# A fused attention and two-layer MLP kernel: wider conversion of second-layer weights, float32 scores of two heads, one mask on VectorE

## The chip, the core and the metric

The kernel runs on one core of a Trainium2 chip. The metric is the device time of one execution in microseconds (us), as the median of several runs. One profiled execution gives the trace. TensorE is PE in the profile (PEld its weight loads), VectorE is DVE, ScalarE ACT, GpSimd POOL, and SyncE, which issues the transfers, SP. Each engine works through its instructions in the order in which the program emits them.

## The reference

Three stages follow one another on 4 x 576 = 2304 tokens of width 512:

```python
scores = q @ k.T / 8                          # 4 batches, 8 heads, 576 x 576, head_dim 64
scores = where(0 <= i - j < 128, scores - slope[h] * |i - j|, -1e9)
x = softmax(scores) @ v                       # heads side by side: 2304 x 512
h = x @ w_in;  x = (h * clip(h + 3, 0, 6) / 6) @ w_out          # d_ff 2048
h = x @ w_in2; out = (s * max(h, 0)**2 + b) @ w_out2            # d_ff 2048
```

All inputs are float32. The weights arrive as 64-bit values (two 32-bit words each), and the kernel turns them into float32 itself.

## The kernel before

**Order of the work.** Everything is entered into a table `plan` by `at(slot, rank, fn)`. At the end the functions are called by slot, and within a slot by rank. This order is the order on every engine; nothing moves an instruction later. Two slots belong to one step `(t, f)` of the first layer: token group `t` (0 to 7; groups 0 to 3 have 256 tokens, the first two query blocks of a batch; groups 4 to 7 have 320, the other three blocks) and 128 columns `f` of d_ff (0 to 15). `hslot` and `oslot` (L80 to L83) give the slots of a step's two products. Groups 0 and 1 are interleaved; group 2 begins at slot 77, group 3 at 109, group 4 at 141, 5 at 173, 6 at 205, 7 at 237 (`last`), and the second layer at 271 (`base`).

**First layer.** A product in near-float32 precision is made of three products of float32r parts: each operand is a rounded part and a remainder. `Step.h` (L597) makes 12 instructions into the single PSUM bank `h`; `relu` on ACT (L608), `product` on DVE (L611), `hi` on ACT (L618) and `lo` on DVE (L622) make the operand of `Step.o` (L635), again 12 instructions, one step later. The next step's `h` needs the bank, which is free once `product` has read it. `Step.end` sends a group's result to DRAM (`x2d`). First-layer weights are converted by `Half` in slots up to about 70.

**Attention.** It runs ahead of the first layer: the eight heads of group g are spread over the 32 slots that end some four slots before group g begins, four slots to a head. For groups 0 and 1 (`StartUnit`) a float32 product on 64 partitions for each of two heads makes the scores (L501). For the others (`Unit`) ACT rounds scaled queries and keys (`casts`, L306 and L307), DVE and POOL make the remainders (`rests`, L311, L316), and two float32r products on 128 partitions make each square of scores (L335). Then: minimum on DVE (L351, L352), exponential on ACT (L362), normalization on POOL (L378), transposition on PE (L387), copy on ACT (`fold`, L391), and the two triangles of each 128 x 128 block by selects on POOL (`masks`, L403). The product with the values (L418) and its rounding (L429, L433) come once for two heads. Score, transpose and value tiles take turns in PSUM banks by `bank` (L131): three of them from slot 23 on.

**Second-layer weights.** The second layer multiplies by a scheme of seven block products, so the weights are not only converted but also combined. One `Pair` (L682) handles 2 x 128 rows of `w_in2` or `w_out2`; there are 16. ACT extracts two parts (L720, L721), DVE shifts and merges the sign (L725, L728), POOL adds (L734), DVE makes four sums (L759), then four times ACT rounds (L770), DVE or POOL makes the remainder (L774), and a store sends both to DRAM (`wh`, `wo`, L784). All use two input buffers in turn and a single `work` tile. The rounded parts are written back into the input buffer, two halves in turn, so the third rounding overwrites what the first store sends. Starts are 7 slots apart, four in each of the groups 3 to 6 (L1100).

**Second layer.** `Tokens` loads `x2d` (L841), forms differences on POOL (L861) and splits them on ACT and DVE (L870, L871). `Inner` and `Tokens.outer` stream the stored weights through a ring of five tiles (`Chunk`) and make the products (L1034, L955). For its first 768 tokens load and splits are planned during group 7.

Of the kernel before, what the change touches and what calls it, by code (L numbers as in the profile page):

```python
# [17 lines left out]
P = 128  # L18
# [5 lines left out]
def tile_alibi_window_attention_moe_moe2(  # L24
# [34 lines left out]
    wpool = layer1.enter_context(tc.tile_pool(name="wpool", bufs=1, side="right"))  # L59
# [27 lines left out]
    warm = wpool.tile([P, 512], BF16, tag="w7", name="warm")  # L87
# [13 lines left out]
    rel0 = rel2[:, P:]  # L101
    s_sb = const.tile([P, 1], F32, name="s_sb")
    b_sb = const.tile([P, 1], F32, name="b_sb")

    def constants():
# [16 lines left out]
        make_identity(nc, ident)  # L122

# [34 lines left out]
    class Half:  # L158
# [18 lines left out]
        def load(self):  # L177
            if self.stage is None:
                raw = raw_half()
            else:  # L180
                raw = wpool.tile(
                    [P, 4 * DM], I32, tag=f"w{self.stage}", name=f"stage{self.id}"
                )[:, : 2 * DM]
# [24 lines left out]
        def hi(self):  # L208
            if self.f not in wt:
                wt[self.f] = wpool.tile(  # L210
                    [P, 2, 2 * DM], F32R, tag=f"w{self.f}", name=f"w1_{self.f}"
                )
# [31 lines left out]
    queries = {}  # L244
    for x in "XY":
        queries[x] = [ap.tile([P, 3 * P], F32R, tag=f"q{x}{i}", bufs=1, name=f"q{x}{i}") for i in (0, 1)]
        for t in queries[x]:
            nc.gpsimd.memset(t[:, S - 2 * P :].bitcast(F32), 0.0)

    def query_tile(x):  # L250
        queries[x].reverse()
        return queries[x][0]

    class Unit:
# [10 lines left out]
        def plan(self, s):  # L265
            two = min(self.qa + 2, self.qb)
            at(s - 7, 1, self.load)
            at(s - 1, 34, self.casts)
            at(s + 1, 33, self.rests)
            at(s + 3, 20, lambda: self.products(self.qa, two))  # L270
            at(s + 4, 20, lambda: self.products(two, self.qb))
            at(s + 3, 32, lambda: self.minima(self.qa, two))
            at(s + 4, 32.7, lambda: self.minima(two, self.qb))
            at(s + 5, 33, lambda: self.exps(self.qa, two))
            at(s + 5, 33, lambda: self.exps(two, self.qb))
            at(s + 6, 32.2, self.sums)
            at(s + 7, 33, self.weights)
            at(s + 9, 20, self.transposes)
            at(s + 9, 35, self.fold)
            at(s + 10, 30.02, self.masks)  # L280
            if self.h % 2:
                at(s + 13, 20, self.values)
                at(s + 14, 39, self.to_hi)
                at(s + 15, 39, self.to_lo)
# [4 lines left out]
        def load(self):  # L289
            i, b = (1, self.b) if self.qa else (0, self.b - NATIVE)  # L290
            raw = ap.tile([P, 768], F32, tag="raw", name=f"raw{self.id}")[:, : self.nq + self.nk]
            nc.sync.dma_start(out=raw, in_=qk[i][b, self.h])
            self.rq = raw[:, : self.nq]
            self.rk = raw[:, self.nq :]
            if self.h % 2 == 0:
                rv = ap.tile([P, 2, 4 * D], F32, tag="v", bufs=3, name=f"rv{self.id}")
                rv = rv[:, :, : self.nkb * D]
                nc.sync.dma_start(out=rv, in_=vv[i][b, self.h // 2])
                for u in self.pair():
                    u.rv = rv[:, u.h % 2].rearrange("p (n d) -> p n d", d=D)  # L300

        def casts(self):
            self.c = -(D ** -0.5) / slopes[self.h]
            self.X = query_tile("X")
            self.C = ap.tile([P, 448], F32R, tag="C", name=f"C{self.id}")[:, : self.nk]
            nc.scalar.activation(self.X[:, : self.nq], self.rq, AF.Copy, scale=self.c)  # L306
            nc.scalar.activation(self.C, self.rk, AF.Copy)  # L307

        def rests(self):
            self.Y = query_tile("Y")  # L310
            nc.vector.scalar_tensor_tensor(  # L311
                out=self.Y[:, : self.nq], in0=self.rq, scalar=self.c,
                in1=self.X[:, : self.nq].bitcast(F32),
                op0=ALU.mult, op1=ALU.subtract,
            )
            nc.gpsimd.tensor_tensor(  # L316
                out=self.C[D:], in0=self.rk[D:], in1=self.C[D:].bitcast(F32), op=ALU.subtract
            )
# [7 lines left out]
        def products(self, a, b):  # L326
            if a == self.qa:
                self.ps = []
            if a < b:
                self.ps.append(bank(f"s{self.id}_{a}"))  # L330
            for i in range(a, b):
                sl, k0, k1 = self.square(i)
                q = (i - self.qa) * P
                for x in (self.X, self.Y):
                    nc.tensor.matmul(  # L335
                        sl,
                        lhsT=x[:, q : q + P],
                        rhs=self.C[:, k0 - self.ka * P : k1 - self.ka * P],
                        start=x is self.X,
                        stop=x is self.Y,  # L340
# [51 lines left out]

# [832 lines left out]
```

## Time and profile before

| | |
|---|---|
| median of 3 runs | 1001.66 us (995.66 to 1003.28) |
| profiled execution | 998.22 us, its span in the trace 996.5 us |
| mean granted TensorE clock | 0.976 of full speed |
| busy: PE, DVE, ACT, POOL | 914.9, 705.5, 529.0, 528.9 us |

The busy time of an engine is summed over the whole span. Matmuls are pipelined, so that a product which waits in the pipe counts as busy. "Idle before, releaser" in a row is the time for which the engine stood still before the instruction, with the instruction that ended it. The granted clock is the share of full speed (2.4 GHz) at which the chip let TensorE run in a stretch.

Where rows are cut by time, the columns are: stretch in us, its length, busy us of PE, PEld, DVE, ACT and POOL (each with its instructions), granted clock, share of the DMA engines, GB/s. The stretches of rows 1 begin with the first `h` product of a token group.

### The profile page before, as it was taken

The numbers are of one execution on the slowest core, as the hardware profiler recorded it, in microseconds if no ns is written. First come the engines' busy times: TensorE is split into PE (matmuls) and PEld (weight loads), VectorE is DVE, ScalarE is ACT, GpSimd is POOL, SyncE is SP. The second block draws the span as 40 slices with busy tenths as digits, with TensorE's granted clock in tenths as the row PEclk, the third lists the DMA queues.
The fourth block names the chain that finished last, engine by engine and source line by source line (L and its number), as shares of the span: only waits on it lengthen the run. The fifth ranks groups of instructions, "written<-read, shape, count | busy, mean of one in ns | idle before, by whom it ended". The sixth has DMA issues, their size and how long they took to land.

```text
span 996.5 us, 18129 instructions
## 1 busy us (share of the span) xinstructions
PE 914.9 (92%) x6517; PEld 868.1 (87%) x6517; DVE 705.5 (71%) x1489; ACT 529.0 (53%) x1283; POOL 528.9 (53%) x685
## 2 busy tenths in 40 slices
PE   9898999997788889878899989999799997999998
PEld 4697899996778878768788989999699997999998
DVE  7999975566766667577675462778956789667693
ACT  7977864455555555546555332555324554336541
POOL 6646753445775576477554130338922479223772
PEclk9999999999989999899999999999999999999999
DMA  9425532244655555454734610987379873797863
GB/s 332 138 77 189 170 96 66 79 136 156 217 176 185 206 176 200 159 178 141 243 135 172 252 59 1 341 282 256 125 266 342 280 276 108 269 326 243 275 227 133
DMA packets 61130, 191.50 MB, mean 192 GB/s; under 512 B 6384, under 2 KB 17776, under 8 KB 52592
## 3 DMA queue, kind: packets, MB, share of 16 engines
q1 hardware_dynamic: 61040, 190.34, 55.6%
q8 instruction: 51, 0.84, 0.3%
q14 instruction: 39, 0.32, 0.1%
HBM read 151.52 MB, written 38.80 MB: 191 GB/s over the span
## 4 chain that ended last, share of the span: by engine, by line
PE 56%; DVE 16%; DMA 10%; ACT 7%; POOL 6%; issue 4%; SPq 1%; ACTq 0%; POOLq 0%; DVEq 0%
PE h L1034 17%; PE o L955 14%; PE h L597 12%; PE o L635 9%; DMA wh<-raw 3%; DVE i L938 3%; DVE work L759 2%; DMA raw<-w 2%; POOL P L378 2%; DMA wo<-raw 2%; PE v L418 2%; POOL work L734 2%; ACT P L362 1%; POOL W L403 1%; DVE g L622 1%
## 5 line engine op out<-in xcount | busy, mean ns | idle before, releaser
L597 PE MATMUL h<-x,w 128*128 128x256 f32 (+1 forms) x1536 | 239.8, 307 | 37.0 <-DVE t L611 36.4
L597 PEld LDWEIGHTS h<-x,w 128*128 128x128 f32 x1536 | 220.7, 197 | 44.6 <-DVE t L611 43.4
L635 PE MATMUL o<-g,w 128*128 128x256 f32 (+1 forms) x1536 | 235.2, 302 | 10.1 <-ACT g L618 5.8
L635 PEld LDWEIGHTS o<-g,w 128*128 128x128 f32 x1536 | 213.3, 192 | 14.6 <-ACT g L618 7.9
L955 PE MATMUL o<-wstream,i 128*128 128x256 f32 x1512 | 184.8, 284 | 13.8 <-DVE i L938 13.5
L955 PEld LDWEIGHTS o<-wstream,i 128*128 128x128 f32 x1512 | 183.0, 192 | 15.4 <-DVE i L938 15.4
L1034 PE MATMUL h<-x,wstream 128*128 128x384 f32 x864 | 154.2, 335 | 0.0
L1034 PEld LDWEIGHTS h<-x,wstream 128*128 128x128 f32 x864 | 150.4, 188 | 0.0
L403 POOL TENSOR_SCALAR_AFFINE_SELECT W<-F 128x128 f32<-128x128 f32 (+1 forms) x240 | 78.3, 364 | 116.1 <-ACT F L391 114.5
L622 DVE TENSOR_TENSOR g<-t,g 128x256 fp32r<-128x256 f32 (+1 forms) x128 | 74.1, 579 | 59.8 <-ACT g L618 59.6
L608 ACT ACTIVATE t<-h 128x256 f32<-128x256 f32 (+1 forms) x128 | 52.1, 407 | 115.1 <-PE h L597 115.0
L611 DVE SCALAR_TENSOR_TENSOR t<-t,h 128x256 f32<-128x256 f32 (+1 forms) x128 | 57.4, 449 | 69.0 <-ACT t L608 68.4
L938 DVE TENSOR_TENSOR i<-g,i 128x768 fp32r<-128x768 f32 x60 | 95.7, 1650 | 6.0 <-issue 4.9
L770 ACT ACTIVATE raw<-work 128x512 fp32r<-128x512 f32 x64 | 36.6, 573 | 97.1 <-DVE work L759 55.6
L949 POOL TENSOR_TENSOR g<-g 128x768 f32<-128x768 f32 x36 | 86.5, 2428 | 0.0
L378 POOL TENSOR_SCALAR P<-P,st 128x128 f32<-128x128 f32 x128 | 67.5, 542 | 3.7 <-DVE st L372 1.9
L1067 POOL TENSOR_TENSOR g<-g 128x384 f32<-128x384 f32 x24 | 22.6, 940 | 82.8 <-ACT g L1063 82.8
L618 ACT ACTIVATE g<-t 128x256 fp32r<-128x256 f32 (+1 forms) x128 | 56.1, 438 | 19.5 <-DVE t L611 19.4
L1071 ACT ACTIVATE g<-g,b_sb,s_sb 128x384 f32<-128x384 f32 x96 | 62.7, 698 | 3.8 <-DVE g L1058 3.8
L316 POOL TENSOR_TENSOR C<-raw,C 64x448 fp32r<-64x448 f32 (+1 forms) x48 | 53.0, 1103 | 15.1 <-issue 6.3
L1079 POOL TENSOR_TENSOR i<-g,i 128x384 fp32r<-128x384 f32 x24 | 24.8, 1034 | 67.2 <-ACT i L1075 67.2
L1058 DVE SCALAR_TENSOR_TENSOR g<-g 128x384 f32<-128x384 f32 x72 | 55.6, 772 | 2.5
(115 smaller groups left out, 1413.6 us busy)
## 6 DMA issues: line engine op xcount, KB each, us to landing
wstream<-wo SPq DMA_DIRECT2D x42, 1024.0 KB, 4.9
raw<-w SPq DMA_DIRECT2D x53, 512.0 KB, 5.6
wstream<-wh SPq DMA_DIRECT2D x24, 1024.0 KB, 5.5
wstream<-wh SPq DMA_DIRECT2D x24, 768.0 KB, 5.6
raw<-qk SPq DMA_DIRECT2D x32, 384.0 KB, 3.1
wh<-raw SPq DMA_DIRECT2D x24, 512.0 KB, 4.6
wo<-raw SPq DMA_DIRECT2D x24, 512.0 KB, 3.3
stage<-w SPq DMA_DIRECT2D x11, 512.0 KB, 5.7
```

The costliest lines, as they stand in the source:

```text
L378: nc.gpsimd.tensor_scalar(out=pt, in0=pt, scalar1=self.st[:, 2, li : li + 1], scalar2=1.0, op0=ALU.mult, op1=ALU.mult,)
L403: nc.gpsimd.affine_select(out=self.W[:, o : o + r], in_=self.F[:, q : q + r], fill=0.0, base=k - 1, compare_op=ALU.is_ge, pattern=[[s, r]] ...
L597: nc.tensor.matmul(self.ps, lhsT=w[:, wp, cc * P : (cc + 1) * P], rhs=x[:, cc, xp], start=m == 0, stop=m == 3 * CC - 1,)
L611: nc.vector.scalar_tensor_tensor(out=self.a, in0=self.a, scalar=6.0, in1=self.ps, op0=ALU.min, op1=ALU.mult)
L618: nc.scalar.activation(self.g[:, 0], self.a, AF.Copy)
L622: nc.vector.tensor_tensor(out=self.g[:, 1], in0=self.a, in1=hi, op=ALU.subtract)
L635: nc.tensor.matmul(acc[t][d], lhsT=w[:, wp, DM + d * P : DM + (d + 1) * P], rhs=self.g[:, gp], start=f == 0 and i == 0 and (t > 1 or d % 2 ...
L938: nc.vector.tensor_tensor(out=out[:, :, 1], in0=src, in1=out[:, :, 0].bitcast(F32), op=ALU.subtract)
L949: nc.gpsimd.tensor_tensor(out=out, in0=a, in1=b, op=op)
L955: nc.tensor.matmul(self.acc[k][c], lhsT=g[:, gp, c * P : (c + 1) * P], rhs=w[:, wp * HB : (wp + 1) * HB], start=p == 0 and i == 0, stop=p ...
L1034: nc.tensor.matmul(ps, lhsT=w[:, wp, cc], rhs=x[:, cc, xp], start=start and m == 0, stop=m == 5, skip_group_check=True,)
L1071: nc.scalar.activation(g, g, AF.Identity, scale=s_sb, bias=b_sb)
```

## The change

- **Conversion (`Pair`).** Its steps are spread over nine slots after its start instead of seven, each in a slot of its own, with ranks of 37 and above for the late ones (behind the step's own instructions at 30 to 32). Starts are 10 slots apart; the first two are at slots 76 and 96, the other 14 from slot 113 to 243. The first two stores leave from a staging buffer of their own (in the attention's pool, at the end in `x1`); only the third and fourth write into the input buffer. DVE makes the first and third remainder, POOL the second and fourth (the other way round before), and the order of the four parts changes.
- **Scores of groups 2 to 7.** Queries and keys of two heads lie on the two halves of the partitions. ACT scales both heads' queries in one instruction, and float32 products on 64 partitions make the scores. The casts and remainders are gone. A pair of heads is planned together, with the odd head's later steps one or two slots after the even head's. Values are loaded on their own, later.
- **Masks.** The lower triangle of the first two blocks of a unit is made by one DVE product of the transposed weights in PSUM with a constant triangle of ones. The other selects stay on POOL.
- **Pools.** First-layer weights 0 to 7 lie in a pool that closes after step (7, 7); tokens, their splits and the fifth ring tile are placed accordingly. `Step.end` writes from tiles `y` of its own, not from conversion buffers. `W` has 3 buffers (4 before), `v` 2 (3 before). The first four weight chunks are loaded from slot 253 on (240 before), the load of the second layer's first tokens is planned at slot 238 (245 before) and their splits are spread out.

```diff
         def plan(self, s):
             two = min(self.qa + 2, self.qb)
...
+            odd = self.h % 2
+            s -= 4 * odd
+            if not odd:
+                at(s - 7, 1, self.load)
+                at(s + 1, 1, self.load_values)
+                at(s - 1, 34, self.scale)
+                at(s + 3, 20, lambda: self.scores(self.qa, two))
+                at(s + 7, 20, lambda: self.scores(two, self.qb))
+            at(s + 3 + 2 * odd, 32, lambda: self.minima(self.qa, two))
+            at(s + 7 + odd, 32.7, lambda: self.minima(two, self.qb))
+            at(s + 5 + odd, 33, lambda: self.exps(self.qa, two))
+            at(s + 8 + odd, 33, lambda: self.exps(two, self.qb))
+            at(s + 9 + odd, 32.2, self.sums)
+            at(s + 10 + odd, 33, self.weights)
+            at(s + 12 + 2 * odd, 20, self.transposes)
+            at(s + 12 + 2 * odd, 35, self.fold)
+            at(s + 12 + 2 * odd, 35, self.lower)
+            at(s + 13 + 2 * odd, 30.02, self.masks)
+            if odd:
+                at(s + 17, 20, self.values)
...
         def load(self):
...
+            n = (self.qb - self.qa) * P
+            raw = ap.tile([P, 832], F32, tag="raw", name=f"raw{self.id}")[:, : n + self.nk]
+            if self.nq < n:
+                nc.gpsimd.memset(raw[:, self.nq : n], 0.0)
+            for u in self.pair():
+                u.p = slice((u.h % 2) * D, (u.h % 2 + 1) * D)
+                src = qk[i][b, u.h, u.p]
+                nc.sync.dma_start(out=raw[u.p, n:], in_=src[:, self.nq :])
+                nc.sync.dma_start(out=raw[u.p, : self.nq], in_=src[:, : self.nq])
...
+        def scale(self):
+            j = self.h // 2
+            nc.scalar.activation(self.q, self.q, AF.Copy, scale=qscale[:, j : j + 1])
...
-                for x in (self.X, self.Y):
+                for u in self.pair():
+                    sl, k0, k1 = u.square(i)
+                    q = (i - self.qa) * P
                     nc.tensor.matmul(
...
+                        sl, lhsT=u.X[:, q : q + P], rhs=u.rk[:, k0 - self.ka * P : k1 - self.ka * P],
+                        start=True, stop=True,
                     )
...
+        def lower(self):
+            self.W = ap.tile([P, 640], F32, tag="W", bufs=3, name=f"W{self.id}")
+            w = self.W[:, : 4 * P].rearrange("p (i k n) -> p i k n", i=2, k=2)
+            ps = self.pt[:, : 2 * P].rearrange("p (i n) -> p i n", i=2)
+            nc.vector.tensor_tensor(
+                out=w[:, :, 1], in0=ps, in1=tri[:, None, :].to_broadcast([P, 2, P]), op=ALU.mult
+            )
...
 class Pair:
...
         def plan(self, s, load):
+            self.s = s
             at(load, 1, self.load)
             at(s, 30.1, self.high)
-            at(s, 38, self.sign)
-            at(s + 1, 31, self.add)
-            at(s + 2, 31.2, self.sums)
+            at(s + 1, 30.1, self.rest)
+            at(s + 1, 38, self.shift)
+            at(s + 2, 38, self.sign)
+            at(s + 3, 31, self.add)
+            at(s + 4, 37, lambda: self.sums(0))
+            at(s + 5, 37, lambda: self.sums(2))
...
-                k = s + (2, 3, 5, 6)[j]
+                k = s + (4, 5, 7, 8)[j]
                 idx = [order.index(x) for x in products]
-                at(k, 31.3, lambda a=(j, src): self.hi(*a))
-                at(k + 1, 31.4, lambda a=(j, src): self.lo(*a))
-                at(k + 1, 31.5, lambda a=(j, idx): self.store(*a))
+                at(k, 37.3, lambda a=(j, src): self.hi(*a))
+                at(k + 1, 37.4, lambda a=(j, src): self.lo(*a))
+                at(k + 1, 37.5, lambda a=(j, idx): self.store(*a))
...
+        def target(self, j, n):
+
+            whole = staging(self.s) if j < 2 else self.raw.bitcast(F32)
+            return whole[:, j % 2 * 2 * DM : j % 2 * 2 * DM + n * DM]
...
-            (nc.gpsimd, nc.vector)[j % 2].tensor_tensor(
+            (nc.vector, nc.gpsimd)[j % 2].tensor_tensor(
                 out=lo.bitcast(F32R), in0=src, in1=hi, op=ALU.subtract
             )
...
-    starts = [hslot[t, 0] + 5 + 7 * i for t in range(3, 7) for i in range(4)]
+    first = hslot[3, 0] + 4
+    starts = [76, 96] + [first + 10 * i for i in range(2 * NP - EARLY)]
     for i, s in enumerate(starts):
-        Pair(i, i % NP, i // NP).plan(s, max(s - 5, starts[i - 2] + 8 if i > 1 else 0))
+        Pair(i, i % NP, i // NP).plan(s, s - 5)
...
         if t == 0:
-            p = last + 10
-            u.plan_input(last + 8, [p, p + 1, p + 2, p + 4, p + 6, p + 8, base + 1], [p + 2, p + 3, p + 5, p + 7])
+            load, p = last + 1, last
+            splits = {1: 5, 5: 9, 7: 13, 3: 20, 6: 24, 2: 25, 4: 29}
+            sums = {5: 7, 7: 10, 6: 21, 4: 26}
...
-    ready = (last + 3, last + 3, last + 4, last + 5, base + 1)
+    done = starts[-1] + 10
+    half = oslot[nt1 - 1, NF // 2 - 1] + 2
+    ready = (done, done, done, done, max(done, half))
```

## Rows read from the trace of the kernel before

**Rows 1.** Busy time (instructions) by engine, PEclk granted clock; cut at token groups 2 to 7

```profile
155.95:211.58 55.63, 55.63 (x474) 53.88 (x473) 30.22 (x115) 28.54 (x100) 23.34 (x58) 1.00 0.27 85
211.58:296.34 84.76, 69.00 (x523) 63.72 (x522) 59.77 (x166) 45.55 (x129) 53.39 (x91) 0.92 0.52 174
296.34:384.71 88.37, 75.98 (x523) 71.52 (x521) 61.46 (x168) 49.05 (x134) 55.93 (x92) 0.96 0.53 182
384.71:475.44 90.73, 77.37 (x522) 72.35 (x521) 61.94 (x167) 49.20 (x134) 56.80 (x92) 0.94 0.53 181
475.44:556.58 81.14, 72.60 (x494) 68.41 (x493) 51.77 (x125) 43.69 (x108) 41.92 (x68) 0.96 0.50 175
556.58:626.15 69.57, 66.44 (x434) 65.63 (x433) 32.28 (x49) 22.35 (x47) 9.92 (x5) 0.98 0.32 114
```

**Rows 2.** The same view, two stretches of groups 0 and 1

```profile
31.42:77.00 45.58, 41.29 (x323) 36.64 (x322) 43.92 (x98) 38.44 (x92) 20.85 (x25) 1.00 0.37 116
77.00:155.95 78.95, 74.21 (x598) 69.18 (x596) 65.30 (x179) 60.03 (x169) 50.26 (x78) 1.00 0.45 139
```

**Rows 3.** Waits, 211.58 to 618 us: engine and line, releaser, total us, times, longest

```profile
ACT raw L770 <- DVE work L759: 55.6, 16, 4.9
...
PE h L597 <- DVE t L611: 32.4, 18, 3.9
ACT raw L770 <- DMA wh<-raw: 25.1, 10, 3.8
...
ACT raw L770 <- DMA wo<-raw: 16.4, 10, 4.0
```

**Rows 4.** The chain that ended last, 296.3 to 330 us: start us, us, what

```profile
305.71 1.77 PE h L597 x12
...
313.34 1.86 POOL work L734
...
315.85 1.24 DVE work L759 x3
...
317.54 3.53 PE h L597 x12
...
324.23 4.60 DMA wh<-raw
```

**Rows 5.** Groups of instructions, whole span: count, busy us, mean ns, idle before

```profile
L403 POOL TENSOR_SCALAR_AFFINE_SELECT W<-F 128x128 f32<-128x128 f32 (+1 forms) x240 | 78.3, 364 | 116.1 <-ACT F L391 114.5 <-ACT g L618 1.1
...
L316 POOL TENSOR_TENSOR C<-raw,C 64x448 fp32r<-64x448 f32 (+1 forms) x48 | 53.0, 1103 | 15.1 <-issue 6.3 <-POOL P L378 6.0
...
L311 DVE SCALAR_TENSOR_TENSOR qY<-raw,qX 128x320 fp32r<-128x320 f32 (+1 forms) x48 | 34.6, 720 | 0.0
...
L759 DVE TENSOR_TENSOR work<-work 128x256 f32<-128x256 f32 x64 | 33.1, 546 | 14.8 <-POOL work L734 13.7
...
L774 DVE TENSOR_TENSOR raw<-work,raw 128x512 fp32r<-128x512 f32 (+1 forms) x32 | 24.1, 753 | 1.6 <-ACT raw L770 1.5
...
L728 DVE SCALAR_TENSOR_TENSOR raw<-raw,work 128x1024 int32<-128x1024 int32 x16 | 19.7, 1232 | 0.5
...
L433 DVE TENSOR_TENSOR x<-v,x 128x256 fp32r<-128x256 f32 (+1 forms) x32 | 14.4, 449 | 0.0
...
L725 DVE TENSOR_SCALAR work<-work 128x1024 int32<-128x1024 int32 x16 | 11.5, 718 | 3.8 <-ACT work L720 3.6
```

**Rows 6.** Instructions in order of time at the two kinds of score products

```profile
8.64 0.93 PE L501 MATMUL s<-raw 64*128 64x128 f32 x8
9.50 1.90 PE L93 MATMUL warm_ps<-warm 128*128 128x512 bf16 x8
...
249.51 0.33 SPq L292 DMA_DIRECT2D raw<-qk  x1
249.54 0.39 PE L335 MATMUL s<-C,qX 128*128 128x256 f32 x1 [1.42 <-POOL C L316]
...
250.12 1.10 PE L635 MATMUL o<-g,w 128*128 128x256 f32 x8
```

More of the change, by code (lines that the diff above doesn't have):

```diff
@@ L122, in constants @@
         make_identity(nc, ident)
+        nc.gpsimd.memset(tri, 1.0)
+        nc.gpsimd.affine_select(
+            out=tri, in_=tri, fill=0.0, compare_op=ALU.is_ge, base=0,
+            pattern=[[1, P]], channel_multiplier=-1,
+        )
+        for h in range(H):
+            c = -(D ** -0.5) / slopes[h]
+            nc.gpsimd.memset(qscale[h % 2 * D : (h % 2 + 1) * D, h // 2 : h // 2 + 1], c)
     def scalars():
@@ L266, in plan @@
             two = min(self.qa + 2, self.qb)
[L267 to L284, printed above, removed]
+            odd = self.h % 2
[18 more added lines that the diff above has]
+                at(s + 17, 20, self.values)
+                at(s + 18, 39, self.to_hi)
+                at(s + 19, 39, self.to_lo)
         def pair(self):
@@ L324, in square, with scores @@
             return self.ps[(i - self.qa) // 2][:, o : o + k1 - k0], k0, k1
[L326 to L330, printed above, removed]
+        def scores(self, a, b):
+            for u in self.pair():
+                if a == self.qa:
+                    u.ps = []
+                if a < b:
+                    u.ps.append(bank(f"s{u.id}_{a}"))
             for i in range(a, b):
-                sl, k0, k1 = self.square(i)
-                q = (i - self.qa) * P
-                for x in (self.X, self.Y):
+                for u in self.pair():
+                    sl, k0, k1 = u.square(i)
+                    q = (i - self.qa) * P
                     nc.tensor.matmul(
[L336 to L340, printed above, removed]
+                        sl, lhsT=u.X[:, q : q + P], rhs=u.rk[:, k0 - self.ka * P : k1 - self.ka * P],
+                        start=True, stop=True,
                     )
@@ L669, in work, with staging @@
         return late["work"]
+    def staging(s):
+        k = "early" if s + 6 < last else "late"
+        assert k == "early" or s + 4 >= last
+        if k not in late:
+            pool, tag = (ap, "stage") if k == "early" else (xpool, "x1")
+            late[k] = pool.tile([P, 4 * DM], F32, tag=tag, bufs=1, name=f"staging_{k}")
+        return late[k]
     HORDER = (1, 5, 6, 7, 3, 2, 4)
@@ L740, in block, with sums @@
             return t[:, i * DM + j * HB : i * DM + (j + 1) * HB]
[L742 removed]
+        def sums(self, first):
             L, S = ({(i, j): self.block(x, i, j) for i in (0, 1) for j in (0, 1)} for x in "LS")
@@ L829, in load @@
         def load(self):
-            if self.t == 0:
-                self.raw = [
-                    wpool.tile([P, 2, TT], F32, tag=f"w{i}", name=f"xr0_{i}") for i in (0, 1)
-                ]
-            else:
-                self.raw = late["xr"]
+            self.raw = late["xr"]
             a = self.t * TT
@@ L876, in plan_input @@
             at(load, 1, self.load)
-            for s, product in zip(splits, FORMS):
+            for product, s in splits.items():
                 at(s, 72.2, lambda n=product: self.split(n))
-            for s, product in zip(sums, (5, 7, 6, 4)):
+            for product, s in sums.items():
                 at(s, 72.5, lambda n=product: self.sum(n))
@@ L1133, in tile_alibi_window_attention_moe_moe2, with tiles, blocks, tokens_pool @@
         at(chunks[before].last + 1 if before >= 0 else ready[c.i], 0.5, c.load)
-    def late_pool():
-        attn_ctx.close()
-        pool = ctx.enter_context(tc.tile_pool(name="late", bufs=1, reuse_waits="tile"))
-        late["xb"] = {k: pool.tile([P, 2, 2, N2], F32R, name=f"x{k}", tag=f"x{k}") for k in FORMS[:-1]}
-        late["t4"] = pool.tile([P, 2, N2], F32, name="t4")
+    def tiles(pool, n, name, shape, dtype=F32):
+        return [pool.tile([P, *shape], dtype, name=f"{name}{i}", tag=f"{name}{i}") for i in range(n)]
+    def blocks(pool, products):
+        for k in products:
+            late["xb"][k], = tiles(pool, 1, f"x{k}_", (2, 2, N2), F32R)
+    def tokens_pool():
+        attn_ctx.close()
+        pool = ctx.enter_context(tc.tile_pool(name="tokens", bufs=1, reuse_waits="tile"))
+        late["xr"] = tiles(pool, 2, "xr", (2, TT))
+        late["xb"] = {}
+        blocks(pool, (1, 5, 7, 6))
+    def more_pool():
+        first_weights.close()
+        late["p"] = ctx.enter_context(tc.tile_pool(name="more", bufs=1, reuse_waits="tile"))
+        blocks(late["p"], (3, 2, 4))
     def second_pool():
```

141 lines of the change are left out of this document (51 added, 90 removed).

## The prediction

> **What bounds the kernel now.** I began with the busy times of all engines in stretches cut at the first `h` product of each token group. PE is the engine that has to be kept busy, but what it loses differs by stretch [rows 1]. Group t=2 takes 55.63 us with PE busy in all of it, at a granted clock of 1.00. Group t=3 runs the same 16 steps on as many tokens and takes 84.76 us, of which PE is busy in 69.00, at 0.92. The difference is that the conversion of second-layer weights (`Pair`) begins there. No other engine is full in t=3 to t=6: DVE is busy for 59.77 of 84.76 us and 61.46 of 88.37, ACT and POOL for less. So the loss is an order of waits, not a lack of engine time.
>
> The loss is idle time of PE plus (1 - granted clock) x stretch, since after idling PE is granted less clock and the next 12 products take 3.53 us where 12 of the same kind took 1.77 shortly before [rows 4]. From rows 1: t=3 15.8 + 6.8 = 22.5 us; t=4 12.4 + 3.5 = 15.9; t=5 13.4 + 5.4 = 18.8; t=6 8.5 + 3.2 = 11.8; t=7 3.1 + 1.4 = 4.5. **Together 73.5 us.** It is a low figure, because a product that waits counts as busy: t=3 lies 29.1 us above t=2, of which its wider scoring explains some 4 by estimate (a third tile for each of 8 heads, at 0.29 us for its two score instructions [rows 6] and as much again for its transpose and values), so 25 against the 22.5. I take 76, and 83 as the upper end (2.5 more in each of four groups).
>
> The waits say why [rows 3]. PE waits 32.4 us for `t` at L611, the DVE product that frees the single bank `h`. Behind that stands ACT, in order: it waits 55.6 us at L770 for the sums of L759, and 25.1 + 16.4 us at the same line until a store of the half it is about to overwrite has landed. The chain shows it [rows 4]: ACT does L720 and L721 back to back, POOL adds at L734, DVE sums, and only then comes the DVE product that PE stands for; a little later a store of 4.60 us holds L770, and everything queued behind it on ACT.
>
> **The change, part by part.**
>
> *Conversion.* The chain of one `Pair` is spread from 7 slots to 9, a step per slot, with 10 slots between starts instead of 7, and its late steps get ranks behind the step's own relu, product and rounding. The first two stores leave from a separate staging buffer, so no write waits for a store of its own conversion: the 41.5 us of DMA waits at L770 go. The 55.6 us go if the sums, a slot ahead now, are done when ACT comes to L770; what is late next is then POOL's add, which waits for the sign step at the end of the slot before. Two conversions move to t=2 and two into t=7. The count of instructions is the same; DVE gets the first and third rounding remainder, POOL the second and fourth. DVE spends (33.1 + 19.7 + 11.5 + 24.1)/16 = 5.5 us on a conversion [rows 5], and a remainder of 512 columns in place of one of 256 adds about 0.5.
>
> *Scores.* Per head the casts and remainders go: DVE 34.6 us, POOL 53.0 us over 48 heads [rows 5], and two ACT copies for each head, of which one scale per pair comes back; ACT is nowhere the fullest engine in rows 1, so I price it at nothing. On PE four instructions that make two squares of one head take 0.58 us from their first start to the start of what follows, so 1.16 for two heads. The start-up units already do float32 products of two heads: 8 instructions for 768 columns take 0.86 us [rows 6], so 1024 columns about 1.15. Nothing is gained or lost on PE. Loads become four small ones per pair instead of two: two more issues at 0.33 us [rows 6] x 24 pairs = 16 us of SP's queue over 400 us, ahead of stores and weight loads which are planned five slots early; nothing. The memset of the padding is one small POOL instruction for every qa=2 pair, on a queue that loses far more.
>
> Between products on 64 partitions and products on 128, PE may lose a gap. From the rows: a lone product of 256 columns lasts 0.39 us and four in a row take 0.58 from start to start, so letting the pipe run empty exposes at most some 0.25 us. 40 calls of `scores` (16 pairs twice, 8 once) with a switch on either side make 40 x 2 x 0.25 = 20 us at most. Against it, the 8 instructions at start-up show no gap: the next kind starts 0.86 us after the first, with the last of them still in the pipe [rows 6]. I take 2 us, near that row, and keep 0 and 20 as ends. The Trainium skill, "TensorEngine Tiling (Array Packing)", section "Tiling Modes", has a rule that speaks against this part: changing the tiling mode drains TensorE. By it the term would be nearer to 20 than to 2; the row does not agree so far.
>
> *Masks.* 96 of 240 selects leave POOL: 96 x 0.364 = 35 us [rows 5]. DVE gets 48 products from PSUM with a broadcast 0/1 tile. None is in the trace; the nearest is L433 (PSUM and SBUF operands, 0.449 us). Ends: a quarter of L725 (1024 columns, one tensor, 0.718), so 0.18, and L759 (two tensors, 0.546) [rows 5]: 9 to 26 us in all; I take 48 x 0.45 = 21.6, since L433 is the only one with an operand in PSUM. So DVE's net over all heads is 21.6 - 34.6 = -13 us.
>
> *Tokens of t=0.* Their load is planned 7 slots earlier and six of seven splits over 20 slots instead of 8, so ACT and DVE no longer take several in a row between two steps; what this returns is part of the 4.5 us of t=7.
>
> **What stays.** DVE's demand by group (8 heads: -5.8 + 3.6; conversions 4 x 5.5 = 22 become 3 or 3.2 x 6.0): t=3 53.6 us, t=4 56.5, t=5 56.9, t=6 45.8, t=2 42, t=7 44. Against the stretches without their losses (62, 72.5, 72, 69, 55.6, 65) it is busy 86, 78, 79, 66, 76 and 68%. How much PE idles beside a DVE so full is read from stretches without `Pair`: 54% goes with 0 (t=2), 83% with 4.74 of 78.95 us = 6%, 96% with 9.4% [rows 1, 2], all at clock 1.00. Between these points by straight lines: 4.2 + 3.6 + 3.7 + 1.7 + 2.6 + 1.9 = 17.7 us. **Sum:** 998.2 (profiled execution; span 996.5) - 76 + 17.7 + 2 = **942 us**. That execution lies 3.4 us under the median of three, whose spread is 7.6; I leave the 942.
>
> The second layer from 626 us on has the same instructions, so I price it at nothing; its cover is that its first weights, loaded at slot 253 instead of 240, still have 18 slots of 1.77 us = 32 us to land.
>
> **The rivals.**
>
> 1. *Stalls remain.* The waits are renamed: conversion bursts on DVE still come between two `h` products, and half of 76 stays: 998 - 38 = 960, spread 952 to 980. For: DVE at 86% in t=3, and two operations of over 1 us in a conversion. Against: adding up the planned instructions at mean durations, DVE exceeds PE over two slots by 0.8 us at most, where before it did by 1.5 us several times in 32 slots. 0.17.
> 2. *The floor.* POOL loses 53 + 35 us, and DVE operations that stretch beside other work shorten (three of L759 in a row took 1.24 us [rows 4], 0.41 each, against a mean of 0.546 [rows 5]); no stall stays: 998 - 83 + 2 = 917, up to 926. 0.12.
> 3. *Gaps at the switches.* The pipe runs empty before and behind each call of `scores`, at the full 20 us: 942 + 18 = 960. The two shapes alternate, which speaks for it; that rows 6 show no gap speaks against. 0.08.
> 4. *Given back at the end of the first layer.* The last two conversions, the splits and the first weights meet in t=7; if the last stores slip, the second layer starts up to 20 us late: 962. For: t=7 gets 12 us more of DVE. Against: there is no attention in t=7. 0.07.
> 5. *Slower: the three score banks.* A pair now takes two of the three banks at once, and the second is freed only by a minimum two slots later; conversions of first-layer weights, transposes and values draw from the same three. PE, in order, then waits for DVE at each of 24 pairs. It ends slower than before from (76 - 18)/24 = 2.4 us per pair on, slower by 1% from 2.8; at 3.3 us it gives 1021. PE's longest wait for DVE at L597 now is 3.9 us [rows 3]. Against: each bank asked for has its last reader at least one slot earlier in the plan, with 2.9 to 3.5 us of `o` and `h` products between. 0.05.
>
> **How the numbers follow.** Forecast (927 to 951) 0.51, and the rivals' chances as given. Range 922 to 966: it leaves out about half of the floor, rival 5 and the worse part of rivals 1 and 4, some 0.2. Some 1% (10 us) is what a measurement of this kernel can tell from no change. Faster by more: all but rival 5 and the far end of rival 1, 0.92; within: 0.03; slower: 0.05.
>
> **What would show it.** In the changed profile: t=3 to t=6 at a granted clock near 1.00 and 62 to 76 us each; no DMA among what L770 waits for; PE's wait for L611 in that stage under 12 us; POOL under 450 us busy and DVE some 700; t=2 up by 2 to 3 us. Wrong if PE waits before the score products for a bank, if the first `h` products of the second layer wait for weights, or if t=3 stays over 75 us.

## The result and the profile after

The changed kernel takes 951.59 us (median of 4 runs, 950.18 to 953.08) against 1001.09 us before: a ratio of 0.951, 95% interval 0.947 to 0.956. Forecast were 942 us, in a range of 922 to 966. The profiled execution has a span of 948.5 us (996.5 before) and a mean granted clock of 0.994 (0.976 before).

The stretches of token groups 2 to 7, each from its first `h` product on, in the columns of [rows 1]; the last line runs to shortly after the start of the second layer:

```profile
161.20:224.75 63.55, 59.33 (x476) 53.78 (x475) 41.54 (x132) 33.33 (x101) 19.06 (x42) 1.00 0.39 129
224.75:290.07 65.32, 63.56 (x523) 57.39 (x521) 48.25 (x155) 38.89 (x115) 31.84 (x68) 1.00 0.50 161
290.07:364.81 74.74, 73.36 (x522) 66.74 (x521) 52.91 (x161) 42.17 (x118) 33.98 (x69) 1.00 0.50 172
364.81:440.51 75.70, 73.80 (x522) 66.92 (x521) 51.80 (x161) 43.81 (x119) 34.75 (x71) 1.00 0.51 170
440.51:511.29 70.78, 68.81 (x492) 64.28 (x491) 47.11 (x122) 36.16 (x93) 29.65 (x52) 1.00 0.51 175
511.29:577.00 65.71, 64.88 (x432) 63.99 (x431) 38.66 (x63) 26.89 (x54) 15.82 (x10) 1.00 0.43 160
```

Groups 3 to 6 took 345 us before [rows 1] and take 286.5 now, at a clock of 1.00. But group 2 begins 5.2 us later than before and takes 7.9 us longer.

The waits of 211 to 575 us, as in [rows 3]:

```profile
PE h L605 <- DVE t L619: 8.2, 14, 1.2
...
ACT staging_late L792 <- DVE work L777: 1.8, 1, 1.8
...
ACT staging_early L792 <- DVE work L777: 1.4, 4, 0.5
```

PE's wait for the product fell from 32.4 us to 8.2. The rounding of weights (L770 before, L792 now) waits for sums 3.2 us in all, 1.4 of them at this tile and 1.8 at the second staging tile, where it was 55.6, and for no store.

The chain that ended last, 290 to 330 us, as in [rows 4], at its first detour:

```profile
299.74 1.76 PE h L605 x12
301.51 0.34 PE t L388 x3
...
301.87 0.45 ACT F L392
...
302.34 0.04 DVE W L401
...
302.68 1.31 DVE raw L746
303.99 0.41 DVE t L619
...
304.45 2.04 PE h L605 x12
```

The chain now consists of PE's own work almost throughout; its one kind of detour, which these 40 us hold twice (again from 324.8 us), was not in the prediction. PE's transpose releases ACT's `fold` (L392), this the new mask on DVE (L401), and behind the mask stand, in DVE's order, a conversion's sign step (L746, 1.31 us) and only then the product for which PE waits.

### The profile page after: what moved, and what is told of

It reads as the page before. It is cut to its first block, busy times and chain, and to the rows that moved or that the text cites. A ratio compares the mean times of both kernels' runs of the same rounds, so it can differ in the third digit from the quotient of the medians.

```text
span 948.5 us, 17831 instructions
## 1 busy us (share of the span) xinstructions
PE 904.2 (95%) x6514; PEld 847.6 (89%) x6517; DVE 689.2 (73%) x1489; ACT 508.5 (54%) x1211; POOL 427.1 (45%) x563
## 4 chain that ended last, share of the span: by engine, by line
PE 76%; DVE 15%; ACT 4%; issue 3%; DMA 1%; POOL 0%; DVEq 0%; ACTq 0%; POOLq 0%
PE h L605 19%; PE h L1045 18%; PE o L643 16%; PE o L966 15%; PE s L339 3%; DVE i L949 3%; PE v L428 3%; DVE z L212 1%; DVE x L882 1%; PE t L388 1%; DVE t L619 1%; DVE raw L746 1%; DMA wstream<-wo 1%; ACT z L207 1%; ACT F L392 1%
## 5 line engine op out<-in xcount | busy, mean ns | idle before, releaser
L605 PE MATMUL h<-x,w 128*128 128x256 f32 (+1 forms) x1536 | 230.8, 299 | 20.5 <-DVE t L619 19.9
L605 PEld LDWEIGHTS h<-x,w 128*128 128x128 f32 x1536 | 211.4, 190 | 27.6 <-DVE t L619 26.0
L643 PEld LDWEIGHTS o<-g,w 128*128 128x128 f32 x1536 | 209.8, 189 | 16.5 <-issue 9.0
L966 PEld LDWEIGHTS o<-wstream,i 128*128 128x128 f32 x1512 | 185.2, 195 | 14.6 <-DVE i L949 14.6
L1045 PE MATMUL h<-x,wstream 128*128 128x384 f32 x1008 | 175.4, 334 | 0.0
L1045 PEld LDWEIGHTS h<-x,wstream 128*128 128x128 f32 x1008 | 174.7, 188 | 0.0
L413 POOL TENSOR_SCALAR_AFFINE_SELECT W<-F 128x128 f32<-128x128 f32 (+1 forms) x144 | 46.0, 352 | 129.6 <-ACT F L392 127.6
L630 DVE TENSOR_TENSOR g<-t,g 128x256 fp32r<-128x256 f32 (+1 forms) x128 | 70.6, 551 | 14.6 <-ACT g L626 13.6
L379 POOL TENSOR_SCALAR P<-P,st 128x128 f32<-128x128 f32 x128 | 54.9, 444 | 44.6 <-DVE st L373 43.9
L401 DVE TENSOR_TENSOR W<-t,tri 128x256 f32<-128x256 f32 x48 | 20.4, 424 | 55.8 <-ACT F L392 55.5
L392 ACT ACTIVATE F<-t 128x320 f32<-128x320 f32 (+1 forms) x48 | 20.0, 417 | 70.6 <-PE t L388 70.6
L1069 DVE SCALAR_TENSOR_TENSOR g<-g 128x384 f32<-128x384 f32 x72 | 55.5, 770 | 2.5
L363 ACT ACTIVATE P<-P,st 128x128 f32<-128x128 f32 x128 | 50.3, 397 | 4.0 <-DVE st L353 3.4
```

The lines of the kernel that those rows point to most:

```text
L379: nc.gpsimd.tensor_scalar(out=pt, in0=pt, scalar1=self.st[:, 2, li : li + 1], scalar2=1.0, op0=ALU.mult, op1=ALU.mult,)
L605: nc.tensor.matmul(self.ps, lhsT=w[:, wp, cc * P : (cc + 1) * P], rhs=x[:, cc, xp], start=m == 0, stop=m == 3 * CC - 1,)
L630: nc.vector.tensor_tensor(out=self.g[:, 1], in0=self.a, in1=hi, op=ALU.subtract)
L643: nc.tensor.matmul(acc[t][d], lhsT=w[:, wp, DM + d * P : DM + (d + 1) * P], rhs=self.g[:, gp], start=f == 0 and i == 0 and (t > 1 or d % 2 ...
L966: nc.tensor.matmul(self.acc[k][c], lhsT=g[:, gp, c * P : (c + 1) * P], rhs=w[:, wp * HB : (wp + 1) * HB], start=p == 0 and i == 0, stop=p ...
L1045: nc.tensor.matmul(ps, lhsT=w[:, wp, cc], rhs=x[:, cc, xp], start=start and m == 0, stop=m == 5, skip_group_check=True,)
```

## The experiments

The groups in this table begin with their first `h` product; "before t=2" is the time at which group 2 begins. The last column is the median of each kernel's runs with its ratio to the kernel before and the interval.

| us | before t=2 | t=2 | t=3 | t=4 | t=5 | t=6 | whole |
|---|---|---|---|---|---|---|---|
| before | 156.0 | 55.6 | 84.8 | 88.4 | 90.7 | 81.1 | 1001.1 |
| changed | 161.2 | 63.6 | 65.3 | 74.7 | 75.7 | 70.8 | 951.6, 0.951 (0.947 to 0.956) |
| conv_only | 153.0 | 65.1 | 68.3 | 74.8 | 74.6 | 70.7 | 947.8, 0.948 (0.945 to 0.951) |
| attn_only | 162.1 | 58.6 | 79.8 | 81.6 | 81.9 | 80.0 | 988.4, 0.988 (0.985 to 0.990) |
| no_staging | 163.6 | 65.3 | 67.1 | 74.8 | 76.6 | 73.4 | 962.4, 0.962 (0.959 to 0.964) |
| no_early | 162.7 | 58.6 | 68.1 | 76.6 | 76.6 | 70.5 | 955.3, 0.955 (0.952 to 0.957) |
| shifted | 163.9 | 61.8 | 65.3 | 74.7 | 75.7 | 70.7 | 951.6, 0.951 (0.949 to 0.952) |
| one_pass | 162.0 | 62.0 | 62.9 | 71.3 | 72.2 | 68.9 | 937.3, 0.936 (0.935 to 0.938) |
| masks_pool | 157.2 | 60.8 | 63.9 | 72.5 | 73.2 | 68.9 | 936.3, 0.935 (0.934 to 0.937) |
| conv_late_parts | 153.0 | 55.6 | 67.5 | 73.4 | 72.4 | 73.3 | 936.4, 0.936 (0.934 to 0.938) |
| lower_later | 156.2 | 61.1 | 64.0 | 72.5 | 73.2 | 68.9 | 936.3, 0.936 (0.934 to 0.938) |
| masks_pool_shifted | 157.8 | 61.5 | 63.8 | 72.5 | 73.2 | 68.9 | 937.9, 0.938 (0.936 to 0.940) |

### Which part brings the gain: conv_only and attn_only

conv_only is the changed kernel with the attention of before; its values are loaded late as in the changed one.

```diff
     class Unit:
...
-        def scale(self):
...
-        def scores(self, a, b):
...
-        def lower(self):
...
+        def casts(self):
...
+        def rests(self):
...
+        def products(self, a, b):
...
-            whole = staging(self.s) if j < 2 else self.raw.bitcast(F32)
+            whole = self.raw.bitcast(F32)
```

> The changed kernel with the attention of before (casts, remainders, float32r products, all masks on POOL), with the conversion of the changed one but for its staging buffer, which finds no room beside the old attention: all four stores leave from the input buffer. Theory A (the gain is the order of the conversion's waits; scores and masks give PE nothing and may cost it): t=3 to t=6 at a clock near 1.00, 935 to 960 us. Theory B (the gain is the 35 us of DVE work and 88 us of POOL work that scores and masks take away): the groups stay at 80 us and more, 980 to 1000 us.

attn_only is the kernel before with that class of the changed one.

```diff
     class Unit:
...
-        def casts(self):
...
-        def rests(self):
...
-        def products(self, a, b):
...
+        def scale(self):
...
+        def scores(self, a, b):
...
+        def lower(self):
...
```

> The kernel before with scores, masks and head-pair plan of the changed one; conversion, pools and tokens as before. Theory A: L770 still waits for sums and stores, t=3 to t=5 stay over 80 us, 975 to 1005 us. Theory B: 950 to 965 us. In both, the stretch ahead of t=2 should show the 5 us that the changed kernel loses there (t=2 begins at 161 instead of 156).

Theory A held: conv_only gives 52.7 us, more than the whole change with its 49.5. Besides the conversion it keeps the changed pools, the output tiles `y` and the plan for the second layer's first tokens, and no run takes these apart; group 2 begins 3.0 us earlier than before, and in conv_late_parts too, which has no conversion ahead of group 3, so that much comes from these or from the later loads of the values. Scores and masks alone give 12 us (1.2%, clear of the spread), within the range of theory A for attn_only and short of theory B, though not nothing, as A had it, and group 3 is with 79.8 us just under its 80. The rounding still waits there, for sums 16.7 us and for stores 21.8, and group 2 begins at 162.1 us, as was expected. Group 4 of conv_only, and the waits of 211 to 575 us in it:

```profile
286.37:361.19 74.82, 71.85 (x521) 68.27 (x521) 61.58 (x160) 47.15 (x130) 47.02 (x91) 1.00 0.56 189
```

```profile
ACT raw L789 <- DMA wo<-raw: 22.6, 15, 3.3
...
PE h L602 <- DVE t L616: 3.1, 7, 0.7
```

DVE is busy in group 4 for 61.6 us (61.5 before), POOL for 47.0, and yet the group takes 74.8 us instead of 88.4. So DVE was not too full; the order was wrong. And group 2 in attn_only:

```profile
162.11:220.72 58.61, 58.61 (x476) 53.69 (x475) 29.18 (x116) 25.86 (x88) 10.92 (x36) 1.00 0.22 66
```

This is the price of the new scores on PE. No conversion runs there and PE is busy in all of it, as it was in group 2 before [rows 1]: 58.61 us against 55.63, **3.0 us more for 8 heads**. Where they stand is read by taking each kind of product from its start to the start of the next kind. One place in the kernel before (two blocks of one head), then one in attn_only (two blocks of two heads):

```profile
187.32 1.58 PE L597 MATMUL h<-x,w 128*128 128x256 f32 x12
188.74 0.28 PE L335 MATMUL s<-C,qX 128*128 128x256 f32 x1
...
189.21 1.60 PE L635 MATMUL o<-g,w 128*128 128x256 f32 x12
190.64 1.58 PE L597 MATMUL h<-x,w 128*128 128x256 f32 x12
```

```profile
194.36 1.60 PE L605 MATMUL h<-x,w 128*128 128x256 f32 x12
195.89 1.13 PE L337 MATMUL s<-raw 64*128 64x256 f32 x8
196.96 1.70 PE L643 MATMUL o<-g,w 128*128 128x256 f32 x12
198.50 1.61 PE L605 MATMUL h<-x,w 128*128 128x256 f32 x12
```

The scores of two heads take 1.06 us where they took twice 0.47; `h` before them takes 1.53 where it took 1.42, and `o` behind them 1.54 where it took 1.43. Added up over all of group 2, score products take 0.5 us more (4.9 for 4.4, with one head's third block more in the stretch) and the 16 `h` and 16 `o` 2.4 us more (48.9 for 46.5). Of these 2.4, some 1.1 stand beside score products, the rest beside transposes and values, where the cause stays open.

Beside no_staging, which differs from conv_only in the attention alone, scores and masks cost 14.6 us once the conversion no longer stalls. one_pass and masks_pool look for where that goes.

### The staging buffer: no_staging

```diff
-            whole = staging(self.s) if j < 2 else self.raw.bitcast(F32)
+            whole = self.raw.bitcast(F32)
```

> The changed kernel without the staging buffer: the first and second rounded parts go back into the input buffer, and the third overwrites what the first store sends. Theory A1 (the spread plan is enough: two slots, 4.4 us, pass between first store and third rounding): 950 to 957 us, with less than 8 us of waits for stores. Theory A2 (the staging buffer is what removes the 41.5 us of waits): 965 to 985 us, with over 20 us of them.

Neither, and the most instructive miss: the waits are those of theory A2, but 962.4 us lie between both theories. The waits of 211 to 575 us in this kernel:

```profile
ACT raw L792 <- DMA wo<-raw: 25.5, 13, 3.3
...
ACT raw L792 <- DMA wh<-raw: 16.0, 9, 3.4
```

These are again 41.5 us, as much as before the change. There they belonged to an order that lost some 75 us; here the kernel is 10.8 us slower than with the staging buffer. (In the table it is 13 us; 2.4 of them lie ahead of group 2, before the first store, where the clock was 0.95 in this profile and 0.99 in that of the changed kernel.) A likely reason why the same wait is cheaper is that it stands at rank 37, behind the step's relu and rounding of that slot, and holds up less; no run tries the rank alone.

### The early conversions: no_early

```diff
-    EARLY = 2
+    EARLY = 0
-    starts = [76, 96] + [first + 10 * i for i in range(2 * NP - EARLY)]
+    starts = [first + 9 * i for i in range(2 * NP - EARLY)]
```

> The changed kernel with no conversion ahead of t=3: 16 starts from slot 113, 9 slots apart instead of 10. Theory C (the two early conversions cost the 7.9 us that t=2 is longer than before): t=2 falls from 63.6 to 58 us or less, and t=3 to t=6 rise by 1 us each at most: 944 to 950 us. Theory D (t=2 is longer because float32 scores take more of PE and because of the head-pair plan): t=2 stays at 61 us or more, 951 to 957 us.

Theory C is right on where group 2 loses: it falls from 63.6 to 58.6 us, all PE work. It is wrong on the sum: groups 3 to 6 take 5.2 us more together (291.7 for 286.5), group 7 some 3 more, and the kernel is 3.7 us slower, which is theory D's range. So the two early conversions cost 5 us in group 2 and save more behind it; the closer starts, 9 slots instead of 10, are part of this and were not tried by themselves.

### The length of the products: one_pass

```diff
-  sl, lhsT=u.X[:, q : q + P], rhs=u.rk[:, k0 - self.ka * P : k1 - self.ka * P],
+  sl, lhsT=u.X[:, q : q + P].bitcast(BF16)[:, 1::2],
+  rhs=u.rk[:, k0 - self.ka * P : k1 - self.ka * P].bitcast(BF16)[:, 1::2],
```

> The changed kernel with its score products taken in bfloat16 (the upper halves of the float32 words, read in place), which leaves out the lower bits of queries and keys; shapes, order and count of products stay. Theory H (the float32 products themselves are longer than the float32r ones were, which made PE's work 3 us longer for every 8 heads): PE's work falls by 4 to 5 us for every 8 heads, 930 to 940 us. Theory I (the added PE time is gaps at the switches between products on 64 and on 128 partitions): under 2 us for 8 heads, 943 to 950 us.

The time is theory H's: 14.3 us less, 2 to 3.5 us for each of the groups 3 to 6, in which PE's busy time falls by 3.7, 4.1, 4.1 and 1.9 us where H had 4 to 5. But the run cannot tell H from I: in one pass a pair's products (0.33 us) are also shorter than the float32r ones were (0.94), so it would gain under either theory. It shows what the length of the float32 products costs, not that they are longer than those of before; that is read from group 2 above, and there 0.5 of the 3.0 us are theirs. PE in order of time, first the changed kernel at one pair's two blocks, then one_pass at the same pair:

```profile
316.08 1.13 PE L339 MATMUL s<-raw 64*128 64x256 f32 x8
317.14 2.03 PE L643 MATMUL o<-g,w 128*128 128x320 f32 x12
319.01 1.93 PE L605 MATMUL h<-x,w 128*128 128x320 f32 x12
320.77 0.49 PE L388 MATMUL t<-ident,P 128*128 128x128 f32 x3
321.02 2.00 PE L643 MATMUL o<-g,w 128*128 128x320 f32 x12
322.86 1.92 PE L605 MATMUL h<-x,w 128*128 128x320 f32 x12
```

```profile
310.22 1.92 PE L606 MATMUL h<-x,w 128*128 128x320 f32 x12
312.08 0.40 PE L339 MATMUL s<-raw 64*128 64x256 bf16 x4
312.41 2.02 PE L644 MATMUL o<-g,w 128*128 128x320 f32 x12
```

From the first score product to the next kind it is 1.06 us in float32 and 0.33 in one pass. The switch itself is seen beside it, and stays in one pass: 12 `h` products of 320 columns take 1.76 us when transposes follow (319.01 to 320.77) and 1.86 when a product on 64 partitions follows (310.22 to 312.08); 12 `o` products take 1.87 us behind the scores (317.14 to 319.01). With the places in group 2 above, a switch thus costs some 0.1 us, and not the 0.25 that the prediction set as its end. The Trainium skill, "TensorEngine Tiling (Array Packing)", section "Tiling Modes", says that a change of tiling mode drains TensorE. The trace agrees in that a cost appears beside products on 64 partitions, and not beside the old scores on 128. But `o` takes 1.84 us behind transposes too (321.02 to 322.86), which are on 128 partitions, and no run takes the partitions and the kind of product apart.

### The mask on DVE: masks_pool and lower_later

```diff
-            at(s + 12 + 2 * odd, 35, self.lower)
-                    if (i == 0, i - self.qa < 2)[k]:
+                    if i == 0 and k == 0:
```

> The changed kernel with all masks on POOL by selects, as before; DVE loses 48 products of 0.42 us (20 us), POOL gets 96 selects of 0.35 us (34 us). Theory J (DVE is what PE waits for, so 20 us less on it helps): 945 to 950 us. Theory K (the masks on POOL hold up the values, or POOL's weights add to what the conversion waits for): 955 to 965 us. If it is off every path: 949 to 954 us.

Faster than any theory had it: 15.3 us. PE is busy in all of group 4:

```profile
281.96:354.44 72.48, 72.48 (x523) 66.62 (x521) 50.03 (x154) 41.83 (x119) 35.41 (x87) 1.00 0.54 185
```

The changed kernel's own rows say why. First the mask's instructions (count, busy us, mean ns, idle before), then DVE in order of time at one head of group 5:

```profile
L401 DVE TENSOR_TENSOR W<-t,tri 128x256 f32<-128x256 f32 x48 | 20.4, 424 | 55.8 <-ACT F L392 55.5
```

```profile
396.25 0.43 DVE L401 TENSOR_TENSOR W<-t,tri 128x256 f32<-128x256 f32 x1 [1.68 <-ACT F L392]
396.59 1.31 DVE L746 SCALAR_TENSOR_TENSOR raw<-raw,work 128x1024 int32<-128x1024 int32 x1
397.82 0.47 DVE L619 SCALAR_TENSOR_TENSOR t<-t,h 128x320 f32<-128x320 f32 x1
```

DVE stands idle for 1.68 us with a sign step ready behind the mask (its last input was done at 393.8 us), then does mask, sign step and product in a row. Work that could have filled the idle time is pushed in front of the product. lower_later keeps the work and moves only its place:

```diff
-            at(s + 12 + 2 * odd, 35, self.lower)
+            at(s + 13 + 2 * odd, 32.1, self.lower)
```

> The changed kernel with the mask on DVE one slot later, behind that slot's product (rank 32.1) instead of at rank 35 of the slot of the transposes. The work on DVE stays the same 20 us. Theory N (the mask costs 15 us because DVE, in order, waits 55 us in all at L401 for PE's transpose and ACT's fold, with the conversion's steps of that slot queued behind it, and these then push the next product): 936 to 942 us, and the wait at the mask falls below 20 us. Theory O (it is the 20 us of work on DVE, or its reading PSUM beside ACT, wherever it stands): 947 to 953 us.

Theory N. The same 48 instructions now wait for nothing:

```profile
L400 DVE TENSOR_TENSOR W<-t,tri 128x256 f32<-128x256 f32 x48 | 20.1, 418 | 0.0
```

PE's wait for the product, from 30 to 575 us, is first the changed kernel's, then that of lower_later:

```profile
PE h L605 <- DVE t L619: 19.9, 24, 2.5
```

```profile
PE h L605 <- DVE t L619: 5.4, 12, 1.5
```

It falls by 14.5 us, and the kernel by 15.3: it takes 936.3 us, as with all masks on POOL. One rank and one slot changed (the selects on POOL, now planned first, take the tile `W`), it beats both kernels by 15 us or more. So the 20 us of DVE work cost no more than the selects on POOL in their stead, and its place cost 15 us.

### The loss ahead of t=2: shifted and masks_pool_shifted

```diff
-            at(s + 5 + odd, 33, lambda: self.exps(self.qa, two))
+            late_by = 0 if self.qa else 1
+            at(s + 5 + odd * (1 + late_by), 33, lambda: self.exps(self.qa, two))
-            at(s + 12 + 2 * odd, 20, self.transposes)
+            at(s + 12 + 2 * odd + late_by, 20, self.transposes)
```

(fold and masks likewise; in masks_pool_shifted on top of masks_pool.)

> The changed kernel with, in the units of groups 2 and 3 alone, the odd head's exponentials one slot later and transposes, fold and masks of both heads one slot later, so that they leave the odd slots in which the conversion of first-layer weights has its work on ACT and DVE. Theory F (the 5 us lost ahead of t=2 is ACT and DVE work bunched in odd slots, which makes the relu and the product of the next slot late): t=2 begins at 154 to 158 us instead of 161, the whole 944 to 948 us. Theory G (rival 5: PE and ACT wait for one of the three PSUM banks, since a pair takes two at once): t=2 begins at 160 to 163, the whole 950 to 953 us.

> The kernel with all masks on POOL (936.3 us) and, in groups 2 and 3, the odd head's exponentials one slot later and transposes, fold and masks of both heads one slot later. Theory F2 (with the mask off DVE, what is left of the loss ahead of t=2 is work of two heads bunched in the odd slots): t=2 begins at 153 to 155 us, the whole 931 to 934 us. Theory G2 (what is left is 3 us of PE work for group 2): t=2 begins at 156 to 158 and the whole is 935 to 938 us.

Theory F fell, and with it F2: group 2 begins at 163.9 and 157.8 us, no earlier than without the shift. That alone does not prove theory G. What is shown is that 4.0 to 5.0 us of the loss were the mask (157.2 without it on DVE, 156.2 with it later, instead of 161.2), and that with the attention of before it is gone (153.0). The rest of 3 to 4 us is not the 3 us of PE work that theory G2 named, though G2's figures came true: from 31.5 us to group 2, PE is busy 1.1 us longer in masks_pool (157.2) than in conv_only, and idle 3.2 us longer. Most of that idle time is theory G's wait for a bank. In masks_pool it comes twice, the second time here:

```profile
117.51 0.48 PE L338 MATMUL s<-raw 64*128 64x128 f32 x2
119.38 0.92 PE L338 MATMUL s<-raw 64*128 64x128 f32 x6 [1.39 <-DVE raw L215]
```

The first head's scores begin, and PE stands before the second head's until L215 has ended: a step of the conversion of first-layer weights that reads `z`, which takes its turn in the same three banks. The two waits are 2.8 us together, and 2.3 in lower_later. The changed kernel has one of 1.1 us; in shifted two come to 3.7. (In lower_later and shifted the view names no releaser, but L215 ends 0.1 us before each.) No run removes them, so what they cost of the whole is not shown.

### Old attention, new order: conv_late_parts

```diff
-    EARLY = 2
+    EARLY = 0
...
-    starts = [76, 96] + [first + 10 * i for i in range(2 * NP - EARLY)]
+    starts = [first + 9 * i for i in range(2 * NP - EARLY)]
...
-                k = s + (4, 5, 7, 8)[j]
+                k = s + (5, 6, 8, 9)[j]
-                parts = (("L", 0), (1, 2)), (("S", 0), (5, 6)), (("S", 1), (7, 3)), (("L", 1, 1), (4,))
+                parts = (("S", 0), (5, 6)), (("S", 1), (7, 3)), (("L", 0), (1, 2)), (("L", 1, 1), (4,))
```

The lines are those against conv_only.

> The attention of before (float32r scores, all masks on POOL), the conversion of the changed kernel without a staging buffer, with 16 starts from slot 113, 9 slots apart, none ahead of t=3, and the four rounded parts in the old order at slots 5, 6, 8 and 9 after the start, so that three slots instead of two lie between the first store and the write over it. Theory L (attention as before costs PE 3 us less for 8 heads and loses nothing ahead of t=2; waits for stores are what the old plan lost): t=2 begins at 153 to 156 and takes 56 us, t=3 to t=6 together 285 to 292, the whole 930 to 940 us, faster than both kernels. Theory M (with old attention and conversions 9 slots apart DVE is too full): t=3 to t=6 together over 297, the whole 943 to 955 us.

Theory L: 936.4 us, with groups 3 to 6 at 286.6 together. Without staging buffer, float32 scores or a mask on DVE it is 15 us faster than the changed kernel, and as fast as lower_later, which has all three. Against conv_only it gains 11.4 us; the starts, the later slots and the order of parts were changed together, and no run takes them apart.

```profile
152.97:208.60 55.63, 55.63 (x474) 53.87 (x473) 30.22 (x115) 28.57 (x100) 23.24 (x58) 1.00 0.27 83
```

Group 2 is back at 55.63 us to the hundredth [rows 1].

## Why the prediction was right, and where its terms were not

- **What bounds the kernel, and the main step.** Right: an order of waits around the conversion, and not a full engine. conv_only shows that the conversion's plan, with the pools that go with it, brings the gain, with DVE as busy as before. That the old order was worth 76 us was not measured by itself. By the prediction's terms (stretch less its loss, plus the straight lines) groups 3 to 6 come to 66.5, 76.1, 75.6 and 71 us; they take 65.3, 74.7, 75.7 and 70.8. Clock, product wait (under 12 us forecast, 8.2 measured) and POOL (427 us, under 450 forecast) came as written.
- **How the waits were weighed.** Half right. The 41.5 us of waits for stores were counted as a cause with the sums; no_staging has the same 41.5 us and loses 10.8. Length is not the price of a wait; what stands behind it seems to be, and for the mask lower_later shows it.
- **The scores on PE.** Mis-sized: taken as 2 us with an end at 20, they are 3.0 us for 8 heads, 18 us of PE work over the 48 heads by proportion (an estimate). The working took four float32r products as 0.58 us from one instance in which the first stood alone, and float32 at 1.15 us as their equal; in group 2, with PE never idle, it is 0.47 and 1.06. That is the smaller part, 0.5 of the 3.0 us. The larger is in `h` and `o`, and about half of it beside the scores: some 0.1 us at a switch. So rival 3 had that part of the mechanism, and its 40 calls with two switches each make 8 us of it; the other half is open. The prediction leaned on the start-up row, in which the next kind starts after 0.86 us; in attn_only such a call is as long (181.69 to 182.55 us), and the cost stands in its neighbours, where that row shows nothing.
- **The mask.** The price of the instruction was right (0.449 taken, 0.424 measured); the step failed in what it left out. The instructions were added to DVE's demand, and not asked what they wait for nor what is queued behind them. DVE idles 55.5 us there, for 15 us of the whole.
- **DVE's fullness as a measure of PE's idling.** The straight lines gave 4.2, 3.6, 3.7 and 1.7 us for groups 3 to 6; PE idles 1.8, 1.4, 1.9 and 2.0. Together they were some 6 us too high, while PE's busy time came out some 3.5 us above the stretches without their losses. That the groups came out right is in part luck, two errors that offset each other.
- **Groups 0 to 2.** Wrong: no change was forecast ahead of group 2, and no reason given for that, and 2.6 us in it; measured 5.2 and 7.9. These 10.5 us are about the 9.6 us between 942 and 951.6. Ahead of group 2 it is mostly the mask's place. In group 2, no_early shows 5.0 us as the early conversions' (saved again elsewhere) and 3.0 as PE work.
- **The rivals.** The wait for the three banks (5), which the prediction named as a sign that it is wrong, did appear, but once at 1.1 us ahead of group 2 and not at each of 24 pairs. Nothing was given back before the second layer (4): from the last step's `h` to the end it is 382.7 us, and was 382.3.

## What to carry to other kernels

Read a wait by what is queued behind it on its engine, and by what waits for that, not by its length: 41.5 us of the same wait cost 11 us in one order and belonged to a loss of some 75 in another, and 55.5 us of idling at the mask cost 15. When an instruction is added to an engine that works in order, ask first what it waits for; an off-path mask of 0.42 us cost 0.3 us each time because it stood ahead of work that was ready, and nothing once it stood behind the product. Price an operation of PE from a stretch in which PE never idles, from start to start and with its neighbours: most of what the new scores cost stood in the products beside them and not in their own. Take work off an engine only where that engine sets the pace: the same scores and masks gained 12 us beside the old conversion and lost 15 beside the new one, about what the mask's place costs.

## What the runs showed of the hardware

The float32 scores of two heads on 64 partitions, 1024 columns in 8 instructions, take 1.06 us; the same products read as bfloat16, in 4 instructions, 0.33 us: 3.2 times as long. Two float32r products on 128 partitions for the same squares took 0.94 us (twice 0.47). So float32 on half the partitions was here no cheaper than two float32r products with their remainders, as far as PE goes. And the 12 products of 256 columns on 128 partitions before and behind such scores took 1.53 and 1.54 us, where they took 1.42 and 1.43 beside float32r scores on 128 partitions.
